# Segment sums of x by matmuls with tile loads, earlier stores of attention outputs, and a denser output projection at the end of attention

## Chip, core and metric

The kernel runs on one NeuronCore of a Trainium2 chip. The metric is the device time of one execution in microseconds (us). Differences of about 0.3% (3.8 us) or less can't be told from no change.

## What is computed

Two independent layers read 2048 tokens of width 1024 each, and their outputs stand side by side in the result.

```
# part A: a diagonal complex state space layer (S5)
Lam_bar = exp(dt * Lam)
Bu = einsum('bld,pd->blp', x, ((Lam_bar - 1) / Lam)[:, None] * Bmat)
for t in range(L):                       # a scan over 2048 tokens
    h = Lam_bar * h + Bu[:, t, :]
y = 2 * einsum('blp,dp->bld', hseq, Cmat).real + x * Dskip

# part B: attention with a recurrent memory; 64 segments of 32 tokens, 8 memory rows, 32 heads of 128
mem = mem0
for s in range(64):
    h = concatenate([mem, x[:, 32 * s:32 * s + 32]])      # 40 rows
    q, k, v = h @ Wq, h @ Wk, h @ Wv
    p = softmax(where(mask, q @ k.T * scale, -1e9))
    o = (p @ v) @ Wo
    mem = o[:, :8]; outs.append(o[:, 8:])
```

Part B's recurrence is broken up in the kernel: it forms a guess of each segment's memory from the segment's mean row of x, computes all segments at once with the guessed rows, compares at the end (`check`), and has a slow general path for inputs for which the guess would not do. The sums of x over each segment of 32 tokens, which this change concerns, feed that guess.

## The kernel before

The work runs in four stages on one core.

**Stage 1** (to about 335 us) interleaves two kinds of steps by the list that `steps()` (L949) makes. A "v" step (`v_x`, L470) multiplies 512 rows of part B's x with a 512-column block of Wv: 32 matmuls of 512 columns into psP, copied out by ScalarE (L89). An "s" step (`stage1`, L257), numbered n = 4 * pc + q from 0 to 31, is one block of part A's scan: 16 matmuls into psU, then on VectorE a product with tables (L268, which frees psU), a sum (L271), two scans (L276), a second product and sum (L287, L288), with ScalarE copies (L277) between and a small carry computed on GpSimd (L281 to L283). SP stores the result (a_hs, L289). After n = 6, 11, 16, 21, 26 and 30 no v step follows, so two scan steps meet there. There are two psU buffers and three psP buffers. In this stage the instructions of TensorE and SP keep the order in which the program writes them (`Pinned`, L54). The order on VectorE, ScalarE and GpSimd comes from a scheduler, except that instructions given to `keep_in_program_order` keep theirs among themselves.

**The segment sums** (`sum_x`, L414) are a generator whose pieces the stage 1 loop (L1028 to L1061) takes one at a time, one for each scan step from n = 3 on. x is viewed as 128 rows of 16 tokens, two rows for each segment. GpSimd issues 16 DMAs, token j of each row into one of two FP32 accumulators (j % 2); from the third on the DMA engines add while they write (L422). Two are issued per step, at n = 3 to 10. VectorE then adds the two accumulators (L427, at n = 11), ScalarE rounds the sum to BF16 (L429), VectorE forms the remainder (L431), and at n = 15 16 matmuls of 64 columns with the indicator `ind` (L107 to L111), two for each of 8 chunks of D, add the two rows of a segment. Four small VectorE instructions (L440 to L443) turn psR into xbar, the mean rows. The tile b_xr holds x rows for the first v step and then the accumulators; the rounded halves and a block of zeros (`fill`, L376) lie in the tile CT, which is loaded with C from n = 17 on.

**og** (L507) multiplies xbar with each Wv block: 32 matmuls of 64 columns into psR. For block 3 it runs at n = 17, and the load of Wv block 5 into the buffer that this frees follows it (L1050 to L1052). For later blocks both follow the block's last v step.

**Stage 2** (to about 460 us) is part A's output product and the guess.

**Attention** (to about 1027 us) goes over 16 head pairs, hp, of 11 units u each. The projections of q and k (`proj`, L587; 18 pieces per pair, 10 pieces ahead) run between the units. A unit has a front (scores on TensorE, exponential on ScalarE L647, mask on GpSimd L650) and a back (weighted values on TensorE, then VectorE L666 and L667 into b_ob), which runs two to three units later. b_ob has 44 blocks per head pair and is filled three blocks at a time. SP stores it to DRAM (b_on, b_tn) when the pair is complete; for the last pair alone (`early`, L671) the first groups are stored once 12 blocks are there. SP also loads the next pair's values (b_v) and the weights b_wq, b_wk. Pins are lifted here, so the scheduler orders all queues.

**Output projection**: when all projections are done, in the last eight units, one step (four matmuls of 512 columns) of `outproj_first` (L754) is taken after each unit (L1136). It has 64 steps: 18 for heads 0 to 23 of three row tiles, then heads 24 to 31, which need the last head pairs (tile b_ol3), and so on. The other three row blocks and the check follow.

Of the kernel before, what the change touches and what calls it, by code (L numbers as in the profile page):

```python
# [8 lines left out]
FP32 = mybir.dt.float32  # L9
BF16 = mybir.dt.bfloat16  # L10
I32 = mybir.dt.int32
ACT = mybir.ActivationFunctionType
ALU = mybir.AluOpType
# [26 lines left out]
EW = E + 8  # L40
# [53 lines left out]
def consts(k):  # L94
    nc, V, G = k.nc, k.V, k.G
    c = k.cst
    k.ident = c.tile([128, 128], BF16, name="ident")
    G.memset(k.ident[:], 1.0)
    G.affine_select(out=k.ident[:], in_=k.ident[:], compare_op=ALU.is_equal, fill=0.0, base=0,
                    pattern=[[-1, 128]], channel_multiplier=1)  # L100
    k.ones = c.tile([128, 1], BF16, name="ones")
    V.memset(k.ones[:], 1.0)
    k.hpb = c.tile([128, 1], FP32, name="hpb")
    k.hpe = c.tile([128, 1], FP32, name="hpe")
    V.memset(k.hpb[:], HALF_PI)
    k.S.activation(k.hpe[:], k.hpb[:], ACT.Exp)
    k.ind = c.tile([128, NSEG], BF16, name="ind")  # L107
    G.memset(k.ind[:], 1.0)
    for base, m in ((0, 1), (1, -1)):
        G.affine_select(out=k.ind[:], in_=k.ind[:], compare_op=ALU.is_ge, fill=0.0, base=base,  # L110
                        pattern=[[-2 * m, NSEG]], channel_multiplier=m)  # L111


def masks(k):
# [223 lines left out]
class PartB:  # L338
# [34 lines left out]
        k.V.tensor_copy(self.memT[:, :, 0:NMX + 1], self.m0T[:])  # L373
        k.V.memset(self.accR[:], 0.0)

    def fill(self, ct):  # L376
        k = self.k
        z = ct[0:32, 0, 2, 0:4 * EW]
        k.V.memset(z, 0.0)
        for hb in range(HB):  # L380
            k.SP.dma_start(self.vx[hb][64 + NMX:GX, :], z[0:GX - 64 - NMX, :])
            k.SP.dma_start(self.vx[hb][T + 32:NSLOT, :], z[0:32, :])
        for q in range(4):
            k.SP.dma_start(self.tn[q][NM:NR, 0:4 * EW], z[0:NR - NM, :])
            k.SP.dma_start(self.tn[q][NM:NR, 1024 - 4 * EW:1024], z[0:NR - NM, :])
# [13 lines left out]
        return [(64 + 1536, 1536, 384), (0, XMAIN, 64), (T - 64, T - 64, 64)]  # L399

    def load_x0(self, tmp, i):
        if i == 0:
            self.x0 = tmp.tile([128, 4, D], BF16, name="b_xr", bufs=1)
        self.k.SP.dma_start(self.x0[:, i, :], self.x[0][64 + 128 * i:192 + 128 * i, :])

    def turn_x0(self, i):

        k = self.k
        pt = k.ps("U", (128, 2, KC, 128), BF16)[:, 0, :, :]
        for c in range(KC):  # L410
            k.PE.transpose(pt[:, c, :], self.x0[:, i, c * 128:(c + 1) * 128], k.ident[:])
        k.copy("vs"[i % 2], self.xe[:, :, 128 * i:128 * i + 128], pt)

    def sum_x(self, tmp, ct):  # L414


        k = self.k; G = k.G
        acc = tmp.tile([128, 2, D], FP32, name="b_xr", bufs=1)
        rows = self.x[0].rearrange("(p j) d -> p j d", j=16)
        for j in range(16):  # L420
            op = {"accum_op": ALU.add} if j > 1 else {}
            k.tc.keep_in_program_order(G.dma_start(acc[:, j % 2, :], rows[:, j, :], **op))  # L422
            if j % 2:
                yield
        s = acc[:, 0, :]
        hl = ct[:, 0, 0:2, :]
        k.tc.keep_in_program_order(k.V.tensor_tensor(s, s, acc[:, 1, :], ALU.add))  # L427
        yield
        k.tc.keep_in_program_order(k.S.activation(hl[:, 0, :], s, ACT.Copy))  # L429
        yield  # L430
        k.tc.keep_in_program_order(k.V.tensor_tensor(hl[:, 1, :], s, hl[:, 0, :], ALU.subtract))  # L431
        yield
        yield
        p = k.ps("R")
        for c in range(KC):
            for i in range(2):
                k.PE.matmul(p[:, c * NSEG:(c + 1) * NSEG], hl[:, i, c * 128:(c + 1) * 128], k.ind[:], start=(i == 0), stop=(i == 1))
        pv = p[:].rearrange("p (c s) -> p c s", c=KC)
        ms = tmp.tile([128, KC], FP32, name="b_ms", bufs=1)
        k.V.tensor_reduce(ms[:], self.m0T[:], AX.X, ALU.add)  # L440
        k.V.tensor_scalar(self.xbar[:], pv, 1.0 / L, None, ALU.mult)
        k.V.tensor_tensor(ms[:], ms[:], pv[:, :, 0], ALU.add)
        k.V.tensor_scalar(self.xbar[:, :, 0], ms[:], 1.0 / L, None, ALU.mult)  # L443
        yield
# [209 lines left out]
    def att_back(self, blocks):  # L654

        k = self.k; PE, V = k.PE, k.V
        hp, b0, n = blocks[0][0], blocks[0][1], len(blocks)
        vt = self.vtile[hp]
        if b0 == 0:
            self.ob = self.p3a.tile([GW, 2 * NG, E], BF16, name="b_ob", bufs=2)  # L660
        o = k.ps(("O", "O", "R")[self.nback % 3], (128, 3, EO))
        self.nback += 1
        for i, (_, b, m, j) in enumerate(blocks):
            PE.matmul(o[:, i, 0:EV], m[:, j * GP:j * GP + 128], vt[:, b // 2, (b % 2) * EW:(b % 2) * EW + EV], start=True, stop=True)
        r = self.accR[0:GW, hp * 2 * NG + b0:hp * 2 * NG + b0 + n]
        V.reciprocal(r, o[0:GW, 0:n, E])  # L666
        V.tensor_tensor(self.ob[:, b0:b0 + n, :], o[0:GW, 0:n, 0:E], r.unsqueeze(2).to_broadcast([GW, n, E]), ALU.mult)  # L667
        q, cs = hp // 4, slice((hp % 4) * 256, (hp % 4) * 256 + 256)
        on, tn = self.on[q], self.tn[q]
        ov = self.ob[:].rearrange("p (g h) e -> p g (h e)", h=2)  # L670
        early = hp == HP - 1  # L671

        def rows(g0, g1):
            r = on[64 + GX * (g0 - 1):64 + GX * (g1 - 1), :].rearrange("(g p) n -> p g n", p=GX)
            k.SP.dma_start(r[:, :, cs], ov[0:GX, g0:g1, :])
        if early and b0 + n == 2 * GE:
            rows(1, GE)
            k.SP.dma_start(on[0:64, cs], ov[0:64, 0, :])
        if b0 + n == 2 * NG:
            del self.vtile[hp]  # L680
            if early:
                rows(GE, NG - 1)
            else:
                rows(1, NG - 1)
                k.SP.dma_start(on[0:64, cs], ov[0:64, 0, :])
            k.SP.dma_start(on[T - 64:T, cs], ov[0:64, NG - 1, :])
            k.SP.dma_start(tn[0:NTL, :].rearrange("(g j) n -> j g n", j=3)[:, :, cs], ov[GX:GW, :, :])
            k.SP.dma_start(tn[NTL:NM, cs], ov[64:64 + NMX, 0, :])
# [292 lines left out]
def kernel_main(tc, A_x, A_Lre, A_Lim, A_Bre, A_Bim, A_Cre, A_Cim, A_logdt, A_Dskip, B_x, B_mem0, B_Wq, B_Wk, B_Wv, B_Wo, out,  # L981
                force=False, dbg=None):
    with ExitStack() as ctx:
        k = K(tc, ctx)
# [15 lines left out]
        with pool("p1x", "right") as p1x, pool("p1", "right", 1) as p1:  # L1000
# [2 lines left out]
            warm(k, p1)  # L1003
            w0 = b.wl.tile([128, KC, 512], BF16, name="b_wv", bufs=2)
            b.load_wv_part(w0, 0, 0, 128, nc.scalar)
            for i in range(4):
                b.load_x0(p1, i)
                if i in (1, 2):
                    b.load_wv_part(w0, 0, 128 * i, (256, 512)[i - 1])
# [12 lines left out]
            b.init(p1)  # L1022
            a.tables(0)
            loads = [[(b, 2)], [(a, 1), (a, 2)], [(b, 3), (a, 3)]]
            sx = b.sum_x(p1, a.CT)
            tabs = {0: a.tabs}
            bts = {0: a.bt}
            for kind, pc, q in order[1:]:  # L1028
                if loads and kind == "v":
                    for o, n in loads.pop(0):  # L1030
                        o.load_x(n)
                if kind == "v":
                    b.v_x(pc, q, wv[pc])
                    if q == 3:
                        if pc > 3:
                            b.og(pc, wv[pc])
                        n = (pc + 2) if pc + 2 < PC else (2, 0)[pc + 2 - PC]
                        if pc != 3:
                            wv[n] = b.load_wv(n)
                    continue  # L1040
                a.tabs, a.bt = tabs[pc], bts[pc]
                n = 4 * pc + q
                if q == 2 and pc + 1 < PC:
                    a.load_b(pc + 1)
                    bts[pc + 1], a.bt = a.bt, bts[pc]
                if pc >= 4 and q == 1:
                    a.load_c(pc - 4)
                if n >= 3:
                    next(sx, None)
                if n == 17:  # L1050
                    b.og(3, wv[3])
                    wv[5] = b.load_wv(5)  # L1052
                a.stage1(pc, q)
                if q == 2 and pc + 1 < PC:
                    a.tables(pc + 1)
                    tabs[pc + 1] = a.tabs
                if n == 12:
                    masks(k)
                    check_consts(k)
                if n == 14:  # L1060
                    b.fill(a.CT)  # L1061
            k.pin.remove("PE")
        psu.close()
        k.psx = ctx.enter_context(tc.tile_pool(name="pss", bufs=1, space=PSUM, reuse_waits="tile"))
# [47 lines left out]
        for n, (hp, u) in enumerate(at):  # L1112
# [13 lines left out]
            if done == 18 * HP:  # L1126
                if first is None:
# [5 lines left out]
                    for h in range(0, H, 16):  # L1133
                        k.SP.dma_start(wo1[:, h:h + 16, :], b.Wo[:, h:h + 16, 512:D])
                    first = b.outproj_first()
                next(first)  # L1136
        p3.close()

# [88 lines left out]
```

## Time and profile before

| | |
|---|---|
| median of three runs | 1258.69 us (1256.14 to 1259.61) |
| the profiled execution | 1256.14 us, its span 1254.4 us |
| granted TensorE clock, mean | 0.997 |
| stage 1, scans under way (36.5 to 334.8 us) | 298.3 us, TensorE busy 288.1, VectorE 255.7 |
| attention, middle (490 to 1012 us) | 522.0 us, TensorE busy 521.6, VectorE 328.1 |
| end of attention (1012 to 1026 us) | 14.0 us, TensorE busy 13.0 |
| output projection (1026 to 1254 us) | 228.0 us, TensorE busy 223.2 |

PE stands for TensorE's matmuls, PEld for its weight loads, DVE for VectorE, ACT for ScalarE, POOL for GpSimd, SP for SyncE (here a queue that issues DMAs). Matmul durations in the rows are latencies, and they overlap: a 512-column matmul has a row of 379 ns, while sixteen follow each other in 3.45 us, 0.216 us apart. A wait is written behind a row in brackets: idle time before the instruction, and the instruction that ended it. The page's own list of the longest idle times before groups has these rows that bear on what follows:

```profile
L64 PE MATMUL psP<-b_wv,b_xe 128*128 128x512 bf16 (+2 forms) x1028 | 225.3, 375 | 7.5 <-ACT b_vst L89 5.8
L64 PE MATMUL psU<-a_xT,a_bt 128*128 128x512 bf16 x499 | 114.8, 380 | 3.6 <-DVE a_pr L268 2.9
b_xr<-in_B_x_dram POOLq DMA_DIRECT2D x16, 512.0 KB, 6.4
b_on<-b_ob SPq DMA_DIRECT2D x15, 960.0 KB
```

The first two are groups (count, busy us and mean ns, idle us before them); the last two are DMA issues (count, KB each, median us from issue to landing where known).

### The profile page before, as it was taken

The page shows a single profiled execution, that of the slowest core. Times are in us where ns is not written, and L with a number is a line of the kernel's source. Part 1 is how long each engine was busy: PE and PEld are TensorE (multiplying, and loading weights), DVE is VectorE, ACT ScalarE, POOL GpSimd, SP SyncE. Part 2 cuts the span into 40 slices and gives each one's busy share as a digit, 9 for nine tenths or more (in the row PEclk, how much of TensorE's full clock was granted, in tenths as well). Part 3 has the DMA queues.
Part 4 walks back from the last instruction along what each step waited for, and adds up shares of the span by engine and source line. Part 5 has one row for each costly group of instructions (what it writes and reads, how often), then busy time and mean ns, then how long its engine had stood idle before and what let it go on. Part 6 is the DMA issues. An engine that isn't in the chain of part 4 may idle for free.

```text
span 1254.4 us, 19885 instructions
## 1 busy us (share of the span) xinstructions
PE 1234.1 (98%) x8159; PEld 659.2 (53%) x8230; DVE 670.0 (53%) x1252; ACT 264.6 (21%) x632; POOL 290.7 (23%) x421
## 2 busy tenths in 40 slices
PE   9999989999999999999999999999999999999998
PEld 4444434444455555566665666565665654446444
DVE  4688699998811124666666666666666641001000
ACT  5344244443320000111211111111211210000000
POOL 4133422212332230222222222232223220000000
PEclk9999989999999999999999999999999999999999
DMA  9978623764698935475454454545474279507000
GB/s 254 230 218 216 179 90 94 194 164 134 166 329 254 276 104 134 122 206 143 107 143 107 114 137 103 129 101 120 95 159 92 60 222 221 125 17 152 17 17 27
DMA packets 316020, 181.00 MB, mean 144 GB/s; under 512 B 138650, under 2 KB 301326, under 8 KB 315926
## 3 DMA queue, kind: packets, MB, share of 16 engines
q1 hardware_dynamic: 291526, 143.75, 46.9%
q10 hardware_dynamic: 21072, 24.38, 5.8%
q0 software_dynamic: 3328, 11.56, 3.4%
q8 instruction: 65, 1.06, 0.4%
q14 instruction: 29, 0.24, 0.1%
HBM read 89.14 MB, written 53.17 MB: 113 GB/s over the span
## 4 chain that ended last, share of the span: by engine, by line
PE 93%; DVE 3%; DMA 3%; issue 1%; POOL 0%; ACT 0%; SPq 0%; DVEq 0%; POOLq 0%
PE psP L64 79%; PE psU L64 7%; PE psS L64 3%; PE psO L64 2%; PE psR L64 1%; DMA b_xr<-in_B_x_dram 1%; DVE a_pr L268 1%; DVE a_pr L276 1%; DMA wo<-in_B_Wo_dram 1%; DMA b_wv<-in_B_Wv_dram 1%; DVE a_pr L271 0%; DVE a_n L287 0%; POOL a_tt L281 0%; POOL a_nx L282 0%; SPq L64 0%
## 5 line engine op out<-in xcount | busy, mean ns | idle before, releaser
L64 PE MATMUL psP<-b_xe,b_wq 128*128 128x480 bf16 (+1 forms) x1280 | 247.7, 343 | 0.1
L64 PE MATMUL psP<-b_xe,b_wk 128*128 128x480 bf16 (+1 forms) x1280 | 247.7, 343 | 0.0
L64 PE MATMUL psP<-b_wv,b_xe 128*128 128x512 bf16 (+2 forms) x1028 | 225.3, 375 | 7.5 <-ACT b_vst L89 5.8
L650 POOL TENSOR_TENSOR b_m<-b_e,maskB 99x396 bf16<-99x396 bf16 x160 | 139.7, 873 | 334.4 <-ACT b_e L647 334.4
L647 ACT ACTIVATE b_e<-psS 99x396 bf16<-99x396 f32 x176 | 88.0, 500 | 532.8 <-PE psS L64 526.7
L64 PEld LDWEIGHTS <-b_wk 128*128 128x128 bf16 x1280 | 119.3, 98 | 94.3
L64 PEld LDWEIGHTS <-b_xe 128*128 128x128 bf16 x1056 | 102.1, 98 | 126.8 <-issue 8.8
L64 PEld LDWEIGHTS <-b_wq 128*128 128x128 bf16 x1280 | 118.6, 98 | 87.8
L91 DVE CAST b_k<-psP 128x480 bf16<-128x480 f32 (+1 forms) x192 | 97.4, 528 | 101.4 <-PE psP L64 101.4
L91 DVE CAST b_q<-psP 128x480 bf16<-128x480 f32 (+1 forms) x192 | 97.4, 528 | 93.0 <-PE psP L64 91.5
L64 PEld LDWEIGHTS <-b_ol 128*128 128x128 bf16 x864 | 84.2, 98 | 94.5
L64 PE MATMUL psU<-a_xT,a_bt 128*128 128x512 bf16 x499 | 114.8, 380 | 3.6 <-DVE a_pr L268 2.9
L64 PE MATMUL psP<-t,a_hl 128*128 128x512 bf16 x496 | 112.1, 379 | 0.8
L91 DVE CAST b_ost<-psP 128x512 bf16<-128x512 f32 (+1 forms) x17 | 11.5, 675 | 183.4 <-PE psP L64 182.4
L64 PE MATMUL psP<-wo,b_ol 128*128 128x512 bf16 (+1 forms) x440 | 91.9, 364 | 0.4
L64 PE MATMUL psP<-t,b_ol 128*128 128x512 bf16 x408 | 91.7, 379 | 0.4
L89 ACT ACTIVATE b_vst<-psP 128x512 bf16<-128x512 f32 x126 | 72.1, 588 | 75.5 <-PE psP L64 63.8
L667 DVE TENSOR_TENSOR b_ob<-psO,b_accR 99x384 bf16<-99x384 f32 x160 | 85.8, 553 | 2.0
L281 POOL TENSOR_SCALAR a_tt<-a_pr,a_tabf 128x1 f32<-128x1 f32 x48 | 34.3, 714 | 226.2 <-DVE a_pr L276 226.2
L64 PEld LDWEIGHTS <-a_bt 128*128 128x128 bf16 x512 | 49.8, 98 | 63.0 <-issue 4.3
L268 DVE TENSOR_TENSOR a_pr<-psU,a_tabf 128x2048 f32<-128x2048 f32 x32 | 73.0, 2282 | 13.5 <-PE psU L64 11.6
L64 PEld LDWEIGHTS <-a_hl 128*128 128x128 bf16 x512 | 49.0, 98 | 56.7
(204 smaller groups left out, 974.0 us busy)
## 6 DMA issues: line engine op xcount, KB each, us to landing
b_v<-b_vx SPq DMA_DIRECT2D x16, 1122.0 KB
b_wv<-in_B_Wv_dram SPq DMA_DIRECT2D x16, 1024.0 KB
b_on<-b_ob SPq DMA_DIRECT2D x15, 960.0 KB
b_vx<-b_vst ACTq DMA_DIRECT2D x24, 544.0 KB
a_hs<-a_h SPq DMA_DIRECT2D x32, 256.0 KB
b_xr<-in_B_x_dram POOLq DMA_DIRECT2D x16, 512.0 KB, 6.4
b_wog<-in_B_Wo_dram SPq DMA_DIRECT2D x4, 2048.0 KB
b_wq<-in_B_Wq_dram SPq DMA_DIRECT2D x16, 512.0 KB
```

Source lines behind the costliest of these rows:

```text
L64: r = f(*a, **kw)
L89: self.S.activation(out, in_, ACT.Copy)
L91: self.V.tensor_copy(out, in_)
L268: V.tensor_tensor(pr[:], u[:].unsqueeze(1).to_broadcast([128, 2, 2, TB]), view(t3, [[TB + 1, 2], [TB + 1, 2], [1, TB]]), ALU.mult)
L276: V.tensor_tensor_scan(w[:, j, :], rb, w[:, j, :], 0.0 if ini is None else ini[:, j:j + 1], ALU.mult, ALU.add)
L281: G.tensor_scalar(tt[:, j:j + 1], w[:, j, TB - 1:TB], t3[:, 1, TB:TB + 1], None, ALU.mult)
L647: k.S.activation(e[:], s[0:GW, :, :, 0:GW], ACT.Exp, scale=float(E) ** -0.5, accum_out=self.accE[0:GW, i:i + 1])
L650: k.G.tensor_tensor(m[0:GW, 0:4 * GP].rearrange("p (a b q) -> p a b q", a=2, b=2)[:, :, :, 0:GW], e[:], mask[0:GW, :, :].unsqueeze(2).to_b ...
L667: V.tensor_tensor(self.ob[:, b0:b0 + n, :], o[0:GW, 0:n, 0:E], r.unsqueeze(2).to_broadcast([GW, n, E]), ALU.mult)
```

## The change

The segment sums are made by TensorE. x is loaded as 16 tiles of 128 tokens (256 KB each) on SP's queue into four buffers of b_xr: four at n = 1, then one after each tile is used. From n = 3 to 10 two tiles are used per scan step: each is, chunk by chunk, the stationary operand of 8 matmuls whose moving operand is an indicator of 4 columns, one for each of the tile's four segments. xbar is made at n = 11 by the same four instructions. The accumulating DMAs and the instructions of L427 to L431 are gone. og for block 3 and the load of Wv block 5 follow that block's last v step, which comes after n = 13. The first v step's x rows are four tiles where they were one.

```
-    k.ind = c.tile([128, NSEG], BF16, name="ind")
-    G.memset(k.ind[:], 1.0)
-    for base, m in ((0, 1), (1, -1)):
-        G.affine_select(out=k.ind[:], in_=k.ind[:], compare_op=ALU.is_ge, fill=0.0, base=base,
-                        pattern=[[-2 * m, NSEG]], channel_multiplier=m)
+    k.ind = c.tile([128, 4], BF16, name="ind")
+    G.memset(k.ind[:], 0.0)
+    for j in range(4):
+        G.memset(k.ind[32 * j:32 * j + 32, j:j + 1], 1.0)
...
-        z = ct[0:32, 0, 2, 0:4 * EW]
+        z = tmp.tile([32, 4 * EW], BF16, name="b_xr", bufs=4)
...
-        if i == 0:
-            self.x0 = tmp.tile([128, 4, D], BF16, name="b_xr", bufs=1)
-        self.k.SP.dma_start(self.x0[:, i, :], self.x[0][64 + 128 * i:192 + 128 * i, :])
+        self.x0.append(tmp.tile([128, D], BF16, name="b_xr", bufs=4))
+        self.k.SP.dma_start(self.x0[i][:], self.x[0][64 + 128 * i:192 + 128 * i, :])
...
-        for j in range(16):
-            op = {"accum_op": ALU.add} if j > 1 else {}
-            k.tc.keep_in_program_order(G.dma_start(acc[:, j % 2, :], rows[:, j, :], **op))
-            if j % 2:
-                yield
-        s = acc[:, 0, :]
-        hl = ct[:, 0, 0:2, :]
-        k.tc.keep_in_program_order(k.V.tensor_tensor(s, s, acc[:, 1, :], ALU.add))
-        yield
-        k.tc.keep_in_program_order(k.S.activation(hl[:, 0, :], s, ACT.Copy))
-        yield
-        k.tc.keep_in_program_order(k.V.tensor_tensor(hl[:, 1, :], s, hl[:, 0, :], ALU.subtract))
-        yield
+        def load(t):
+            if t < TT:
+                xrs[t] = tmp.tile([128, D], BF16, name="b_xr", bufs=4)
+                k.SP.dma_start(xrs[t][:], self.x[0][t * 128:(t + 1) * 128, :])
+        for t in range(4):
+            load(t)
         yield
         p = k.ps("R")
-        for c in range(KC):
-            for i in range(2):
-                k.PE.matmul(p[:, c * NSEG:(c + 1) * NSEG], hl[:, i, c * 128:(c + 1) * 128], k.ind[:], start=(i == 0), stop=(i == 1))
+        for t in range(TT):
+            xr = xrs.pop(t)
+            for c in range(KC):
+                o = c * NSEG + 4 * t
+                k.PE.matmul(p[:, o:o + 4], xr[:, c * 128:(c + 1) * 128], k.ind[:], start=True, stop=True)
+            load(t + 4)
+            yield
...
-                        if pc > 3:
+                        if pc >= 3:
                             b.og(pc, wv[pc])
...
+                if n == 1:
+                    next(sx)
                 if n >= 3:
-                    next(sx, None)
-                if n == 17:
-                    b.og(3, wv[3])
-                    wv[5] = b.load_wv(5)
+                    for _ in range(2):
+                        next(sx, None)
```

Attention outputs are stored in two steps for head pairs 1 to 15, where it was pair 15 alone. And in the last eight units of attention two steps of the output projection are taken after each unit in place of one.

```
-        early = hp == HP - 1
+        early = hp > 0
...
                 next(first)
+                next(first)
```

More of the change, by code (lines that the diff above doesn't have):

```diff
@@ L374, in init, with fill @@
         k.V.memset(self.accR[:], 0.0)
-    def fill(self, ct):
+    def fill(self, tmp):
         k = self.k
-        z = ct[0:32, 0, 2, 0:4 * EW]
-        k.V.memset(z, 0.0)
+        z = tmp.tile([32, 4 * EW], BF16, name="b_xr", bufs=4)
+        k.V.memset(z[:], 0.0)
         for hb in range(HB):
@@ L410, in turn_x0, with sum_x @@
         for c in range(KC):
-            k.PE.transpose(pt[:, c, :], self.x0[:, i, c * 128:(c + 1) * 128], k.ident[:])
+            k.PE.transpose(pt[:, c, :], self.x0[i][:, c * 128:(c + 1) * 128], k.ident[:])
         k.copy("vs"[i % 2], self.xe[:, :, 128 * i:128 * i + 128], pt)
[L414 to L419, printed above, removed]
-        for j in range(16):
-            op = {"accum_op": ALU.add} if j > 1 else {}
-            k.tc.keep_in_program_order(G.dma_start(acc[:, j % 2, :], rows[:, j, :], **op))
-            if j % 2:
-                yield
-        s = acc[:, 0, :]
-        hl = ct[:, 0, 0:2, :]
-        k.tc.keep_in_program_order(k.V.tensor_tensor(s, s, acc[:, 1, :], ALU.add))
-        yield
-        k.tc.keep_in_program_order(k.S.activation(hl[:, 0, :], s, ACT.Copy))
-        yield
-        k.tc.keep_in_program_order(k.V.tensor_tensor(hl[:, 1, :], s, hl[:, 0, :], ALU.subtract))
-        yield
+    def sum_x(self, tmp):
+        k = self.k
+        xrs = {}
+        def load(t):
[4 more added lines that the diff above has]
+            load(t)
         yield
         p = k.ps("R")
-        for c in range(KC):
-            for i in range(2):
-                k.PE.matmul(p[:, c * NSEG:(c + 1) * NSEG], hl[:, i, c * 128:(c + 1) * 128], k.ind[:], start=(i == 0), stop=(i == 1))
+        for t in range(TT):
[5 more added lines that the diff above has]
+            yield
         pv = p[:].rearrange("p (c s) -> p c s", c=KC)
@@ L1005, in kernel_main @@
             b.load_wv_part(w0, 0, 0, 128, nc.scalar)
+            b.x0 = []
             for i in range(4):
@@ L1024, in kernel_main @@
             loads = [[(b, 2)], [(a, 1), (a, 2)], [(b, 3), (a, 3)]]
-            sx = b.sum_x(p1, a.CT)
+            sx = b.sum_x(p1)
             tabs = {0: a.tabs}
@@ L1034, in kernel_main @@
                     if q == 3:
-                        if pc > 3:
+                        if pc >= 3:
                             b.og(pc, wv[pc])
                         n = (pc + 2) if pc + 2 < PC else (2, 0)[pc + 2 - PC]
-                        if pc != 3:
-                            wv[n] = b.load_wv(n)
+                        wv[n] = b.load_wv(n)
                     continue
@@ L1060, in kernel_main @@
                 if n == 14:
-                    b.fill(a.CT)
+                    b.fill(p1)
             k.pin.remove("PE")
```

## The prediction

> **What bounds the kernel now.** I read the page's busy shares first, then a table of stages, then the waits of TensorE, and last the timeline around each long wait.
>
> ```profile
> PE 1234.1 (98%) x8159; PEld 659.2 (53%) x8230; DVE 670.0 (53%) x1252; ACT 264.6 (21%) x632; POOL 290.7 (23%) x421
> ```
>
> TensorE is busy for 1234.1 of 1254.4 us, so only 20.3 us of the span are not its work. The next view, busy time by stage, says where those lie: the stage of part A's scans (67 to 335 us), then the head pairs.
>
> ```profile
> 67.60:143.40 75.80, 75.43 (x346) 34.34 (x352) 61.69 (x54) 31.99 (x57) 30.07 (x44) 1.00 0.83 234
> 143.40:172.00 28.60, 19.84 (x82) 8.41 (x82) 24.35 (x20) 11.26 (x19) 6.05 (x7) 0.88 0.28 84
> 172.00:334.80 162.80, 161.91 (x864) 75.98 (x880) 146.98 (x130) 64.00 (x111) 38.53 (x69) 1.00 0.55 146
> ```
>
> Columns: length, busy time of PE, PEld, DVE, ACT, POOL, granted clock, DMA share, GB/s. One stretch of 28.6 us holds 8.76 us of idle TensorE, and its clock is 0.88; before and after it PE is 99.5% busy. The head pairs are tighter still: from 490 to 1012 us PE is busy for 521.63 of 522.00. The timeline of the bad stretch:
>
> ```profile
> 137.73 0.91 POOL L422 DMA_DIRECT2D b_xr<-in_B_x_dram  x1 [0.92 <-DMA b_xr<-in_B_x_dram]
> 139.58 0.87 POOL L422 DMA_DIRECT2D b_xr<-in_B_x_dram  x1 [0.95 <-DMA b_xr<-in_B_x_dram]
> 143.59 3.62 PE L64 MATMUL psU<-a_xT,a_bt 128*128 128x512 bf16 x16
> 146.64 1.23 DVE L427 TENSOR_TENSOR b_xr<-b_xr 128x1024 f32<-128x1024 f32 x1 [9.16 <-DMA b_xr<-in_B_x_dram]
> 147.78 2.28 DVE L268 TENSOR_TENSOR a_pr<-psU,a_tabf 128x2048 f32<-128x2048 f32 x1
> 150.12 3.61 PE L64 MATMUL psU<-a_xT,a_bt 128*128 128x512 bf16 x16 [2.91 <-DVE a_pr L268]
> 153.57 5.34 PE L64 MATMUL psP<-b_wv,b_xe 128*128 128x512 bf16 x23
> 164.71 3.57 PE L64 MATMUL psP<-b_wv,b_xe 128*128 128x512 bf16 x8 [5.79 <-ACT b_vst L89]
> 168.07 4.01 PE L64 MATMUL psU<-a_xT,a_bt 128*128 128x512 bf16 x16
> ```
>
> VectorE reaches L427, which adds the two accumulators, before the last accumulating transfer has landed, and stands for 9.16 us. Behind it in VectorE's order stands L268, which empties a psU buffer; PE wants that buffer at 147.2 and waits 2.91. The scans run late from there, ScalarE (whose table work waits for VectorE) empties psP late, and PE waits 5.79 more. After that wait matmuls of 512 columns run at half pace: eight take 3.57 us (eight at the usual 0.216 us spacing: 1.73), and by the chain of waits the next sixteen take 3.80 where others take 3.45.
>
> **The change, part by part.** (a) *The accumulating transfers, L427, L429 and L431 go.* The two waits are worth 2.91 + 5.79 = 8.70 us, and the slow matmuls (3.57 - 1.73) + (3.80 - 3.45) = 2.19 us. Would another wait take their place? Without L427 VectorE could start L268 when it fell idle, at 146.64 - 9.16 = 137.5, and free psU at 139.8, 7.4 us before PE asks. In the 162.8 us behind the stall VectorE is 147.0 busy and PE waits for nothing, and at the same meeting of two scan steps at 98.7 us PE ran 32 matmuls on end. So I take all of it: -10.89. Bounds: 0 if something else holds VectorE there, -10.89.
>
> (b) *128 matmuls of 4 columns come, 16 of 64 columns go.* These are on TensorE, which has no cover to give: each ns counts. Each new matmul has its own 128x128 weights. The trace has no 4-column matmul with full weights. Nearest row, the same weights with 64 columns:
>
> ```profile
> 203.46 1.10 PE L64 MATMUL psR<-b_xbar,b_wv 128*128 128x64 bf16 x32
> 204.40 1.89 PE L64 MATMUL psU<-a_xT,a_bt 128*128 128x512 bf16 x8
> ```
>
> From 203.46 to 204.40 are 32 of them: 29.4 ns each, though one weight load lasts 98 ns in its row, so loads overlap. Bounds: below, if spacing went on falling with columns as it does from 99 columns (four in 0.34 us, of which the last is 208 ns: 44 ns) to 64 (29.4), by 0.42 ns a column, 4 columns would take 4.4 ns, 0.6 us in all. Above, if 4 columns hide no load, 98 ns each, 12.5 us. I take 29.4, since a load must already keep that pace: 128 x 29.4 = 3.76 us. The 16 that go took 189.18 to 189.65: -0.47. Net +3.29, between +0.1 and +12.1.
>
> The Trainium skill, "TensorE: Matmul & The Clock Gate", section "LDWEIGHTS (loading the stationary operand)", gives a load its columns divided by 1.2 in ns, 107 ns for 128, and so speaks against this part: 13.7 us for 128 loads, and a sum near +1.4 us where mine is a gain. Its section "Weight-path perf modes" allows a faster load for 128 weights that aren't FP32; the 29.4 ns above side with that.
>
> (c) *Sixteen loads of 256 KB move to SP's queue, behind the a_hs stores there.* A load waits until TensorE is done with the tile four before it; behind it stand that step's a_hs store, the next b_wv load and the a_bt transposes. The stores are read only in stage 2, and the b_wv load for the next column block is queued ahead of the new pair (70.1 against 70.5 us). PE uses a pair two scan steps after its load is queued. From the SP timeline (stores at 69.7, 80.1, 91.6, 100.8, 113.5 us) and PE's steps, the margins are 18, 18, 10, 4, 9 and 14 us. The 4 belongs to the pair queued behind these:
>
> ```profile
> 101.15 2.47 SPq L64 DMA_TRANSPOSE a_bt<-in_A_B_re_dram  x1
> 103.67 4.68 SPq L64 DMA_TRANSPOSE a_bt<-in_A_B_im_dram  x1
> ```
>
> They end at 108.35, PE wants the tiles at 112.5. Landing times on POOL's queue are 5.7 us for 256 KB (a_xn) and 4.6 to 9.4 for the accumulating 512 KB; with 9.4 PE would wait 5.2 us. But the same two transposes took 1.55 and 1.31 us at 59.72, with no accumulating transfers in flight, which is how it will be here; 4.3 us more margin covers 5.7. I take 0, range 0 to 5.2.
>
> The skill's "DMA: Bandwidth & Descriptors", section "Anatomy of one DMA", has 2.0 us plus bytes over 436 GB/s, for 256 KB 2.6 us as an estimate, less than the row; by it the wait is 0 even with the slow transposes.
>
> (d) *og(3) and load_wv(5) move from step 17 to step 13.* The same 32 matmuls; xbar is made at step 11, two steps (some 20 us) ahead. The b_wv buffer comes free earlier, no PE wait hangs on it now. 0. The constant ind and the zero rows of fill are a few small instructions off the path, 0; the cover is that PE runs without them until step 3.
>
> (e) *Early stores for head pairs 1 to 14.* Fourteen more DMA issues, the same bytes. SP spends 0.3 to 2.5 us on a b_on issue, beside 253 us in which it waits for VectorE's b_ob. The early one will wait for the fourth b_ob group; behind it stands the b_wk load for the pair after next (713.47 us), which is read from about 746 (one pair lasts 33.78 us). 0, by that cover of 33 us; without it each us of lateness would cost 14.
>
> (f) *Two steps of output projection per attention unit.* The same matmuls, eight steps earlier. They fill PE's waits for GpSimd in the last units:
>
> ```profile
> 1018.48 0.23 PE L64 MATMUL psO<-b_v,b_m 128*128 128x129 bf16 x1 [0.20 <-POOL b_m L650]
> 1021.45 0.29 PE L64 MATMUL psO<-b_v,b_m 128*128 128x129 bf16 x2 [0.26 <-POOL b_m L650]
> 1025.68 0.29 PE L64 MATMUL psO<-b_v,b_m 128*128 128x129 bf16 x2 [0.44 <-POOL b_m L650]
> ```
>
> One step is four matmuls, 0.86 us, more than each wait: -0.90. What is late next: attention ends 8 x 0.86 = 6.9 us later, so do its last stores and the transposes of the next b_ol (issued 1034.3 to 1051.9, then to 1058.8). Their reader starts when the first block's 64 steps end, near 1075: 16 us of cover. The b_ol3 tile, needed at step 18, is issued at 1016.4 as now and read about 0.9 us sooner.
>
> Sum: -8.70 - 2.19 + 3.29 - 0.90 = -8.5 us. The profiled execution took 1256.14 us (span 1254.4), so 1247.6 on it; it is the lowest of the three runs, and their median is 1258.69, so 1250.2 for a median. I write 1250. With the bounds of (b): -11.7 to +0.3.
>
> **Rivals.** *The wait moves rather than goes* (0.15): the tight pair of (c) lands late by the whole 5.2 us and the slow clock comes with it (2.2): -8.5 + 7.4 = -1.1, 1257.6. For it: the 4 us margin, and VectorE 90% busy. Against: the quick transposes at 59.72.
>
> *Slower: weight loads don't hide under 4 columns* (0.09). If each pair of load and matmul takes the 195 ns of the one-column row (c_one), 128 make 25.0 us: -10.89 - 0.90 - 0.47 + 25.0 = +12.7, 1271. It breaks even at 96 ns a pair and is slower by 0.3% (3.8 us, about what a measurement of this kernel can tell from no change) from 126. Against: the 29.4 ns row. A late b_wk in each pair would need 0.9 us times fourteen to do the same (0.05).
>
> *The split stores do nothing* is part of the forecast, since they end no wait.
>
> **How the numbers follow.** Forecast 0.71, same 0.15, slower 0.14. The forecast's own range is 1247 to 1254 (the bound of -11.7, and +4 for part of a late tile). For eight in ten I go from 1246 to 1259, which takes in the first rival and leaves out the slow one. Faster 0.71, within 0.3% 0.15, slower 0.14.
>
> **What would show it.** No L427 and no VectorE wait on b_xr; PE's 2.91 and 5.79 gone and the clock 1.00 from 143 to 172; 128 rows psR<-ind,b_xr spaced near 29 ns, eight together 0.24 us; no PE wait on b_xr at steps 3 to 10; no POOL waits in the last units. Wrong, if the spacing is near 100 ns or more, or if psU or b_xr waits stand where these were.

## The result, and the profile after

The changed kernel took 1246.9 us (median of four runs, 1246.65 to 1247.2). The kernel before, run again beside it, took 1258.87 (four runs, 1256.14 to 1259.61). The ratio is 0.9909, with an interval of 0.9892 to 0.9926: faster by 0.9%, 12.0 us between the medians. The two profiled executions took 1256.14 and 1246.95 us, their spans 1254.4 and 1245.3, so 9.1 to 9.2 us lie between them, and that is the difference which the traces can explain.

The page of the changed kernel begins with the busy time of each engine and its instruction count:

```profile
PE 1234.2 (99%) x8270; PEld 662.5 (53%) x8342; DVE 667.7 (54%) x1250; ACT 263.4 (21%) x631; POOL 275.8 (22%) x407
```

TensorE is as busy as before (1234.1), in a span that is 9.1 us shorter: what went is idle time, while the new matmuls and the slow ones that are gone about even out. The table by stage says where. Columns as before: length, busy time of PE, PEld, DVE, ACT and POOL, granted clock, DMA share, GB/s.

```profile
67.60:143.40 75.80, 75.37 (x443) 35.84 (x450) 65.97 (x61) 31.50 (x55) 15.52 (x26) 1.00 0.59 177
143.40:172.00 28.60, 28.44 (x159) 13.50 (x161) 26.13 (x25) 12.66 (x22) 7.97 (x10) 1.00 0.19 68
172.00:334.80 162.80, 161.96 (x823) 75.41 (x838) 147.29 (x125) 64.31 (x113) 40.37 (x75) 1.00 0.57 149
...
1012.00:1026.00 14.00, 13.89 (x95) 7.40 (x95) 5.23 (x16) 2.37 (x8) 3.52 (x5) 1.00 1.08 294
```

The stretch from 143 to 172 us, which held 8.76 us of idle TensorE at a clock of 0.88, has 0.16 us at 1.00. In the window from 1012 to 1026 us, which held the end of attention before and now reaches some 5 us past it, TensorE went from 13.0 to 13.9 busy of 14. TensorE's row of time at the meeting of steps 11 and 12, the place of the long waits:

```profile
139.09 7.07 PE L64 MATMUL psP<-b_wv,b_xe 128*128 128x512 bf16 x32
145.99 7.07 PE L64 MATMUL psU<-a_xT,a_bt 128*128 128x512 bf16 x31
152.90 7.07 PE L64 MATMUL psP<-b_wv,b_xe 128*128 128x512 bf16 x31
```

No bracket stands behind any row: 32 matmuls of two scan steps run on end (one record of the 32 is missing), as the prediction took from the meeting at 98.7 us.

The new matmuls, eight for each x tile, two tiles a step:

```profile
66.82 0.54 PE L64 MATMUL psR<-ind,b_xr 128*128 128x4 bf16 x16
67.22 3.61 PE L64 MATMUL psU<-a_xT,a_bt 128*128 128x512 bf16 x16
```

The next matmul starts 0.40 us after the first of the sixteen: 25.2 ns each, with weights of its own for each. And SP's queue at the place where the prediction saw the thinnest margin:

```profile
101.57 1.48 SPq L64 DMA_TRANSPOSE a_bt<-in_A_B_re_dram  x1
103.10 1.32 SPq L64 DMA_TRANSPOSE a_bt<-in_A_B_im_dram  x1
104.52 1.97 SPq L64 DMA_DIRECT2D b_xr<-in_B_x_dram  x2
```

The transposes that took 2.47 and 4.68 us before take 1.48 and 1.32. The two tiles behind them are issued by 106.5 and read at 113.71; TensorE has no wait on b_xr. Its only listed wait in the whole profile is one of 1.3 us at the very start, which the kernel before has too.

### The profile page after: what moved, and what is told of

The parts are those of the page before. It is cut to its first block, busy times and chain, and to the rows that moved or that the text cites. A ratio compares the mean times of both kernels' runs of the same rounds, so it can differ in the third digit from the quotient of the medians.

```text
span 1245.3 us, 20124 instructions
## 1 busy us (share of the span) xinstructions
PE 1234.2 (99%) x8270; PEld 662.5 (53%) x8342; DVE 667.7 (54%) x1250; ACT 263.4 (21%) x631; POOL 275.8 (22%) x407
## 4 chain that ended last, share of the span: by engine, by line
PE 99%; issue 0%; DVE 0%
PE psP L64 82%; PE psU L64 9%; PE psS L64 3%; PE psO L64 2%; PE psR L64 2%; DVE b_xe L91 0%; DVE b_ost L91 0%; DVE a_n L962 0%; DVE hpb L105 0%; DVE ones L102 0%
```

## The experiments

All were timed in three rounds (the last two in five) beside the kernel before on the same chip, whose medians there were 1257.96 (e1 to e4), 1257.15 (e5 to e8) and 1257.2 (e9, e10). A value is a median with its runs' range. The changed kernel itself was timed in an earlier set, beside runs of the kernel before with a median of 1258.87, so differences to its 1246.9 compare runs that were not taken together, and so do those between experiments of different sets (three chips). Only e1 to e4, e5 to e8, and e9 and e10 stand side by side. All differences from here on that are below 3.8 us are small for this measurement; they are taken as real where the ranges of one set don't meet or where the traces show the same.

### Is it the transfers, or where VectorE meets them?

The theory of the prediction: the stall came from L427's place in VectorE's order, before the last accumulating transfer had landed. The rival: the accumulating transfers themselves hold the stage up, so that they have to go. This kernel is the one before with L427 taken after step 11's VectorE work; all accumulating transfers stay.

```
-                if n >= 3:
+                if n >= 3 and n != 11:
                     next(sx, None)
                 ...
                 a.stage1(pc, q)
+                if n == 11:
+                    next(sx)
```

> The kernel before, with one thing changed: the addition of the two accumulators (L427) is traced after scan step 11 instead of before it, so that it stands behind that step's work in VectorE's order; all accumulating transfers stay. Theory (the addition's place makes the stall): VectorE's wait of 9.16 us, TensorE's 2.91 and 5.79 us and the half-speed matmuls after them go, 10.9 us in all: the profiled time falls from 1256.1 to about 1245 to 1246, and the runs come closer together. Rival (the accumulating transfers themselves, or VectorE's load at 90%, hold up the scans): the waits stay, or appear one step later, and the time stays at 1254 to 1259.

Measured: 1248.97 (1247.79 to 1252.57), ratio 0.9932 (0.991 to 0.9955). The timeline of its VectorE, with L427 in its new place:

```profile
157.73 0.68 DVE L288 TENSOR_TENSOR a_h<-a_n 128x1024 bf16<-128x1024 bf16 x1
158.33 1.22 DVE L427 TENSOR_TENSOR b_xr<-b_xr 128x1024 f32<-128x1024 f32 x1
159.47 2.33 DVE L276 TENSOR_TENSOR_SCAN a_pr<-a_rr,a_pr 128x512 f32<-128x512 f32 x2
```

L427 starts 11.7 us later than in the kernel before, with no wait in front, and L268 no longer stands behind it. TensorE in the same stretch:

```profile
136.69 7.07 PE L64 MATMUL psP<-b_wv,b_xe 128*128 128x512 bf16 x31
143.60 7.07 PE L64 MATMUL psU<-a_xT,a_bt 128*128 128x512 bf16 x32
150.51 7.07 PE L64 MATMUL psP<-b_wv,b_xe 128*128 128x512 bf16 x31
...
203.59 1.89 PE L64 MATMUL psP<-b_wv,b_xe 128*128 128x512 bf16 x8 [1.45 <-ACT b_vst L89]
...
221.24 2.12 PE L64 MATMUL psP<-b_wv,b_xe 128*128 128x512 bf16 x9 [1.02 <-DMA b_wv<-in_B_Wv_dram]
```

Both long waits are gone with every transfer still there, so the transfers made the stall only through the place of one VectorE instruction. What remains is smaller: a wait for ScalarE's copies, and 1.02 us for the load of Wv block 5, which SP issues at 213.59, behind og at step 17. With these two waits the expectation was missed in part: the profiled run took 1247.79 where 1245 to 1246 was expected, and the runs lie no closer together (4.8 us apart). Moving that instruction alone in the kernel before is worth 9.0 us; the sums as changed bring 10.3 in the same set (e2 below), and the whole change 12.0 in its own.

### The parts at the end: one step or two, one store or more

Three variants of the changed kernel: the sums alone (attention as before), one projection step with the split stores, and two steps with the split store for the last pair alone.

```
e2 and e4:   -        early = hp > 0
             +        early = hp == HP - 1
e2 and e3:   -                next(first)      (one of the two)
```

> The segment sums as changed, but the output stores and the one output projection step per unit as before. Theory: stall and slow matmuls go (-10.9 us), the matmuls cost 128 x 25.2 ns less the 0.47 us of the old ones (+2.8): about 8 us under the profiled 1256.1, 1248, and some 1 to 2 us above the changed kernel's 1246.9. Rival (a good part of the 12 us comes from the stores or the denser end of attention): 1250 or more.

> The changed kernel with one output projection step per unit, as before. Theory: TensorE waits for GpSimd in the last units again, three or four waits of 0.2 to 0.5 us; 0.9 to 1.8 us above the changed kernel: 1247.8 to 1248.7. Rival (the waits were hidden by something else): 1246.9.

> The changed kernel with only the last head pair stored in two steps, as before. Theory (the split stores end no wait): 1246.9, within 0.4 us. Rival (they spare TensorE the 0.3 us of idle time between 490 and 1012 us, or let the last transposes start earlier): 0.3 to 1 us longer.

| | split stores of pairs 1 to 14 | without them |
|---|---|---|
| two steps | 1246.9 (the change) | 1245.94 (1245.86 to 1246.06), e4 |
| one step | 1248.4 (1248.34 to 1249.03), e3 | 1247.66 (1247.16 to 1248.09), e2 |

The second projection step is worth 1.5 (with the split stores) and 1.7 us (without); the split stores cost 1.0 and 0.7 us. The 1.7 and the 0.7 compare runs of one set whose ranges don't meet; the 1.5 and the 1.0 compare with the changed kernel's own set. Neither the theory nor the rival written down for e4 foresaw that it would be the faster one. Ratios to the kernel before: e2 0.9909 (0.9886 to 0.9932), e3 0.9918 (0.9895 to 0.9941), e4 0.9897 (0.9875 to 0.992). The sums alone are 10.3 us below the kernel before in the same set of runs.

Where the steps' gain comes from is seen in e3's TensorE at the end of attention:

```profile
1008.54 0.28 PE L64 MATMUL psO<-b_v,b_m 128*128 128x129 bf16 x2
1009.02 0.23 PE L64 MATMUL psO<-b_v,b_m 128*128 128x129 bf16 x1 [0.20 <-POOL b_m L644]
...
1011.51 0.22 PE L64 MATMUL psO<-b_v,b_m 128*128 128x129 bf16 x1
1011.99 0.29 PE L64 MATMUL psO<-b_v,b_m 128*128 128x129 bf16 x2 [0.26 <-POOL b_m L644]
...
1015.39 0.39 PE L64 MATMUL psO<-b_v,b_m 128*128 128x129 bf16 x4
1016.22 0.29 PE L64 MATMUL psO<-b_v,b_m 128*128 128x129 bf16 x2 [0.43 <-POOL b_m L644]
```

The three waits for GpSimd are those of the kernel before. What they cost is more than the brackets say. Such matmuls follow each other 0.057 us apart (six in 0.34 in the rows of the changed kernel below), so the third of the first group would have started at 1008.65 and started at 1009.02: 0.37 us lost where 0.20 is written, since a bracket counts from the end of the row before, and the overlap of the two rows is lost as well. The others lose 0.42 and 0.60; together 1.4 us, near the 1.5 to 1.7 measured (e2's profile also has a wait of 0.54 us at 492.84 that e4's lacks, so not all of the 1.7 need be the step's). In the changed kernel the same matmuls stand without a bracket:

```profile
1020.58 0.50 PE L64 MATMUL psO<-b_v,b_m 128*128 128x129 bf16 x6
1020.92 0.28 PE L64 MATMUL psR<-b_v,b_m 128*128 128x129 bf16 x2
1021.03 1.89 PE L64 MATMUL psP<-t,b_wv 128*128 128x512 bf16 x8
```

The price of the split stores is not on any engine. The last VectorE copy of the changed kernel, and below it that of e4:

```profile
1239.32 0.42 DVE L91 CAST b_ost<-psP 128x256 bf16<-128x256 f32 x1 [6.24 <-PE psP L64]
```

```profile
1239.25 0.42 DVE L91 CAST b_ost<-psP 128x256 bf16<-128x256 f32 x1 [6.24 <-PE psP L64]
```

All computation ends within 0.07 us of each other, but the spans end at 1245.3 and 1244.2. The waits of SP's own queue show one at the program's last lines, in the kernel before, the changed kernel and e4, in this order (sum, times, longest):

```profile
SPq L1161 <- SPq L1161: 1.2, 2, 0.7
```

```profile
SPq L1156 <- SPq L1156: 2.8, 1, 2.8
```

```profile
SPq L1156 <- SPq L1156: 1.4, 2, 0.9
```

From the end of the last copy to the end of the span, called the closing here, are 5.6 us in the changed kernel, 5.4 in e3, 4.5 in e2 and e4, and 3.7 to 3.8 in the kernel before and e1 (one profile each).

### Is it the stores, or the number of instructions on SP?

The theory: the closing grows with the number of DMA instructions on SP, wherever they stand. The rival: the stores of attention themselves (late data, late landing) lengthen it. This kernel is e4 with fourteen more DMAs in stage 1, a thousand microseconds before the end: fourteen a_hs stores written as two each.

```
-        k.SP.dma_start(self.hs[tb][:, pc, :, :], h[:])
+        if 12 <= 4 * pc + tb < 26:
+            k.SP.dma_start(self.hs[tb][:, pc, 0, :], h[:, 0, :])
+            k.SP.dma_start(self.hs[tb][:, pc, 1, :], h[:, 1, :])
+        else:
+            k.SP.dma_start(self.hs[tb][:, pc, :, :], h[:])
```

> The changed kernel with only the last head pair stored in two steps (1245.9), and instead 14 of the 32 a_hs stores of stage 1 issued in two halves, so that SP again has 14 DMA instructions more, but not in attention. Theory (the 1 us that the split output stores cost lies behind the last computation and hangs on SP's longer instruction stream): about 1246.9, with 5.4 to 5.6 us from the last VectorE copy to the end instead of 4.5. Rival (it is the output stores themselves, their DMAs or semaphores): 1245.9.

Measured: 1246.82 (1246.71 to 1246.99), 0.88 us above e4 and equal to the changed kernel. Its SP wait at the end:

```profile
SPq L1160 <- SPq L1160: 2.9, 1, 2.9
```

The closing is 5.6 us again, and its last copy starts at 1239.19. So the stores of attention are not needed for it; fourteen more DMA instructions on SP do it by themselves. Nor does it go by the packets that the DMAs moved: the changed kernel has 223 more than e4 and e6 has 2015 more, with 5.6 us in both. Why more instructions on SP make the closing longer isn't shown. The pages give no sign of more pieces of instructions being brought in: their two queues of the kind "instruction" moved 66 and 30 packets in the changed kernel and in e6, 66 and 31 in e4.

### The price of the 4-column matmuls

Each of the 128 matmuls is issued three times and writes the same product each time. If TensorE has slack in this stage, the 256 more cost less than 256 x 25.2 ns = 6.45 us.

```
-                k.PE.matmul(p[:, o:o + 4], ..., k.ind[:], start=True, stop=True)
+                for _ in range(3):
+                    k.PE.matmul(p[:, o:o + 4], ..., k.ind[:], start=True, stop=True)
```

> The changed kernel with each of the 128 matmuls of 4 columns issued three times into the same place (each with its own weight load; the result is the same). Theory (TensorE has no cover to give in this stage, and one pair of load and matmul costs its spacing of 25.2 ns): 256 x 25.2 ns = 6.45 us longer, 1253.4, about twice the price of the sums. Rival (VectorE, 90% busy, leaves TensorE some slack there): clearly less than 6.45 us.

Measured: 1253.32 (1252.97 to 1253.73), 6.42 us above the changed kernel, ratio to the kernel before 0.9968 (0.9957 to 0.9979); that compares two sets, but the traces say the same: from scan step 0 to the last VectorE copy its profile is 6.50 us longer than the changed kernel's. Its timeline at step 3:

```profile
66.95 1.34 PE L64 MATMUL psR<-ind,b_xr 128*128 128x4 bf16 x48
68.16 3.18 PE L64 MATMUL psU<-a_xT,a_bt 128*128 128x512 bf16 x13
```

48 in 1.21 us: 25.2 ns again. Each ns of them counts in full.

### The place of og and of the Wv load

The changed kernel with og for block 3 and the load of Wv block 5 back at step 17.

```
-                        if pc >= 3:
+                        if pc > 3:
                             b.og(pc, wv[pc])
...
+                if n == 17:
+                    b.og(3, wv[3])
+                    wv[5] = b.load_wv(5)
```

> The changed kernel with og for block 3 and the load of Wv block 5 back at step 17. The prediction took this move at nothing: 1246.9, no wait of TensorE on b_wv. Rival (the load had little time to spare before, and the move is part of the gain): a TensorE wait on b_wv of 1 us or more near 220 us, 1248.

Measured: 1247.2 (1246.97 to 1247.91), 0.3 us above the changed kernel, with overlapping ranges, and no TensorE wait on b_wv. The move is worth nothing that these runs can tell; in e1, where SP and TensorE meet a little otherwise, the same late load cost the 1.02 us shown above.

### A version with the accumulating transfers

e1 with the load and og at step 16 and two projection steps: L427 held, no new matmuls, no split stores.

```
-                if n == 17:
+                if n == 16:
                     b.og(3, wv[3])
...
                 next(first)
+                next(first)
```

> The kernel before with the accumulating transfers, L427 traced after scan step 11 (as in the run that showed 1249.0), og for block 3 and the load of Wv block 5 at step 16 instead of 17, and two output projection steps per unit. Theory (what is left over in that run is TensorE's 1.0 us wait for this b_wv load, and the waits of the last units, 1.4 us): about 1246.5, and with no 4-column matmuls perhaps below the changed kernel. Rival (accumulating transfers leave waits that move about from run to run): 1248 or more, with a spread of some us.

Measured: 1245.18 (1245.0 to 1245.62), ratio 0.9903 (0.9887 to 0.992). It is the fastest here, 1.7 us below the changed kernel's median from the other set and 1.6 to 2.0 below e6 and e8 in the same one, though still with TensorE waits that the changed kernel lacks:

```profile
PE psP L64 <- ACT b_vst L89: 1.6, 1, 1.6
PE psU L64 <- DMA b_xr<-in_B_x_dram: 0.9, 1, 0.9
PE psP L64 <- DMA b_wv<-in_B_Wv_dram: 0.5, 1, 0.5
```

The Wv wait at 221 us is gone (the 0.5 is at 9.8 us). It saves the 2.8 us net of the new matmuls, and its closing is 3.75 us long.

### The start-up

Kernels whose first x rows lie in one tile (before, e1, e7) start scan step 0 on TensorE at 36.5 to 36.6 us, those with four tiles at 35.5 to 35.9. In the former the second tile's transposes wait 0.2 to 0.9 us for a load; but two with four tiles have that wait as well, e2 (0.80) and e6 (0.64), and start at 35.86 and 35.51. Two kernels try whether the tiling is the reason: e9 is e4 with the four x0 tiles as slices of one tile again (in the empty C tile), e10 is e7 with the first two as tiles of their own.

```
e9:   -        self.x0.append(tmp.tile([128, D], BF16, name="b_xr", bufs=4))
      +        (self.x0 = a.CT[:, 1, 0:4, :], loaded slice by slice)
e10:  -            self.x0 = tmp.tile([128, 4, D], BF16, name="b_xr", bufs=1)
      +        if i < 2:
      +            self.x0.append(tmp.tile([128, D], BF16, name="b_x0", bufs=2)[:])
```

> The kernel of e4_last_early (1245.94), except that the four x tiles of the first v step are slices of one tile again, here in the still empty C tile. Theory that one tile makes the second tile's transposes wait for a later load: the 0.9 us wait of TensorE on x before the second eight transposes (6.08 us in the kernels with one tile) comes back, the first psU row of scan step 0 stands near 36.5 instead of 35.5 to 35.9, and the time is about 0.7 us higher, 1246.6. Rival, that the start-up differs for another reason (which loads are in flight, where the tile lies): no such wait, 1245.9.

> The kernel of e7_acc_og16 (accumulating transfers kept, L427 behind step 11's VectorE work, og at step 16, two projection steps, early stores for the last pair alone; 1245.18), with the first two x tiles of the first v step as tiles of their own. If tile granularity makes the start-up wait: the 0.9 us wait at 6.08 us goes, psU of scan step 0 starts about 0.7 us sooner, 1244.5. If the start-up differs for another reason: 1245.2.

Measured: e9 1246.71 (1246.23 to 1247.79), e10 1245.48 (1245.36 to 1245.51). The timeline of e9 (the tile is called t there):

```profile
4.43 0.61 PE L64 MATMUL psU<-ident,t 128*128 128x128 bf16 x8
5.74 0.62 PE L64 MATMUL psU<-ident,t 128*128 128x128 bf16 x8 [0.70 <-DMA t<-in_B_x_dram]
...
35.77 3.62 PE L64 MATMUL psU<-a_xT,a_bt 128*128 128x512 bf16 x16
```

The wait came back, but step 0 starts at 35.77, no later than in e4 (35.82): the wait costs nothing there, and e9's 0.8 us more come from elsewhere (its profile has a wait of 0.60 us for ScalarE at 345.64). That its time is near the 1246.6 expected is luck. In e10 the wait shrank to 0.40 us, and step 0 starts at 36.69, no sooner. So the tiles are not the reason.

The traces show the place. In the kernel before and in the changed one these are the 16 matmuls of 256 columns with the second part of Wv, and step 0:

```profile
9.73 1.91 PE L64 MATMUL psP<-b_wv,b_xe 128*128 128x256 bf16 x16 [0.55 <-DMA b_wv<-in_B_Wv_dram]
...
36.54 3.62 PE L64 MATMUL psU<-a_xT,a_bt 128*128 128x512 bf16 x16
```

```profile
8.93 1.91 PE L64 MATMUL psP<-b_wv,b_xe 128*128 128x256 bf16 x16
...
35.74 3.62 PE L64 MATMUL psU<-a_xT,a_bt 128*128 128x512 bf16 x16
```

From the one to the other are 26.81 us in every kernel but e3 (27.18, with a wait of its own), and in before, e1, e7 and e10 alone the chain that ended last goes through the load of Wv that SP issues at 2.84 us; it lands at 9.7 to 9.8 us there. In the other kernels these matmuls start at 8.70 to 9.08 and do not wait for it. Why the load lands later in the four is open; the accumulating transfers, first issued at 68.9 us, can't be the reason.

## Why the prediction came out as it did

The time lay 3.1 us under the predicted 1250, 0.1 us under the forecast's own range (1247 to 1254) and inside the wider one (1246 to 1259), and the forecast's mechanism is the one that acted. On the profiled executions its sum was -8.5 us and the spans give -9.1, but that nearness is partly luck: four terms were off and two parts not foreseen, and they cancel.

**(a), the stall, right in cause and slightly short.** e1 shows the cause by itself: the transfers kept, VectorE's wait gone, both TensorE waits gone, mean clock 1.000. The term -8.70 took the two brackets as they stand. By the count of lost starts that e3's rows show, they cost 3.08 (the first psU matmul could have started at 147.04 and started at 150.12) and 5.96 us, 9.04 together. The slow matmuls' time went as well: none of the three stretches from 67 to 335 us has a clock under 1.00. The prediction's 2.19 for it is a little high, since 3.57 us is a row that holds the last matmul's latency, set against a spacing. From start to start the 8 and the 16 took 3.36 and 3.85 us where 1.73 and 3.45 are usual: 2.03 lost.

**(b), the new matmuls, right in kind, the size 17% too high.** 25.2 ns each where 29.4 were taken, 3.2 us for 128 where 3.76 stood, net of the 16 that went +2.76. e5 shows that the term counts in full. The bound from one load's 98 ns row was far off: the new loads, 96 ns each in their rows, overlap. The Trainium skill's formula for a load ("TensorE: Matmul & The Clock Gate", section "LDWEIGHTS (loading the stationary operand)"; 107 ns for 128 columns as an estimate by it) is not what such a pair costs in these runs, about a quarter of it. The same page's section "Back-to-back issue gap" has a floor of about 25 ns for up to 64 columns, in a table for the matmul without its load; the 25.2 ns of the pairs with 4 columns is as short, while the 29.4 at 64 columns lies above it.

**(c), the tile loads on SP, right, with one thing missed.** The reason given, that the transposes would be quick without accumulating transfers beside them, is what the SP rows show, and e1 (which keeps those transfers) has them slow again, 2.98 and 4.31 us. The skill's section that the prediction quotes here, on the anatomy of one DMA, is on DMAs that GpSimd issues; the tile loads go out on SP, and no row here shows how long they take to land. What was missed stands under (e).

**(d), og and the Wv load moved, right at nothing** in this kernel (e8), with a thin margin: the cover is gone in e1 and costs 1.0.

**(e), the split stores, wrong at nothing.** They cost 0.7 to 1.0 us. The step that failed is "0, by that cover of 33 us": the cover hides the waits, and it did, since TensorE's work ends at the same time with and without them. But the term looked for a cost only among engines that wait, and the cost was in the closing, where more SP instructions make it longer (e6). The sixteen tile loads of (c) seem to pay the same way: 4.3 to 4.5 us of closing in e2, e4 and e9 against 3.7 in the kernel before, though no run took that part out alone.

**(f), two projection steps, mis-sized.** -0.90 was the sum of three brackets; e2 against e4 and e3 against the change give -1.7 and -1.5. The brackets leave out the lost overlap; counted by starts the three waits are 1.4.

**Not foreseen:** 0.8 us at the start, since the first matmuls no longer wait for a load of Wv (why it lands sooner is open), and a wait of TensorE early in attention that the changed kernel does not have, put down to no other engine:

```profile
501.67 0.50 PE L64 MATMUL psO<-b_v,b_m 128*128 128x129 bf16 x6 [0.37 <-issue]
```

Put together on the spans: -9.04 - 2.03 + 2.76 - 1.4 - 0.8 - 0.37 + 1.83 (closing 5.56 against 3.73) = -9.05, against -9.1 measured.

**The step from the profiled run to the median failed by most of what the number missed.** The prediction added 2.55 us because the median of before lay that much above its profiled run, as if the changed kernel would have the same distance. It has none: its runs lie within 0.55 us, at a mean granted clock of 0.999 to 1.000. The runs of before range over 3.5 us beside the changed kernel, over 5.7 beside e1 to e4, there with a clock from 0.994 (the run of 1262.99) to 0.997 (one of 1257.36), and over 1.8 and 1.7 in the two later sets. So the medians are 12.0 apart where the profiled executions are 9.2 apart, and against the medians that before had in the other sets, 1257.15 to 1257.96, the same 1246.9 would be 10.3 to 11.1 below. That the half-pace stretch behind the stall varies from run to run may be the reason, but that is not shown: e1, without that stall, still had runs of 1251.07 and 1252.57 at clocks of 0.998 and 0.997.

**The rivals.** The wait did not move: there is no b_xr wait. A load and its matmul took 25.2 ns together, far from the 96 at which that rival breaks even. And the accumulating transfers need not go for the gain: e7 keeps them and is faster.

## What to carry to other kernels

Before replacing a mechanism that an engine waits for, move the waiting instruction in that engine's order: one VectorE instruction that starts 11.7 us later brought 9.0 us where the whole rewriting brought 12.0 in its own set, and the version built on it (e7) came out 1.7 us under the rewritten one. Size a wait by the start that the pipelined instruction would have had, not by the printed idle time, which here was 0.17 us short at each wait. And cost added DMA instructions at the end of the program as well as where they stand.

## What the runs showed of the hardware

- Matmuls of 4 columns, each with its own 128x128 BF16 weights, followed each other at 25.2 ns, with 48 on end as with 16, while the row of one of these loads lasts 96 ns.
- Fourteen more DMA instructions on SP lengthened the closing by 0.9 to 1.1 us (4.5 to 5.4 or 5.6 us from the last copy to the end of the span), whether they stood in stage 1 or in attention.
- The same pair of DMA transposes took 1.48 to 1.50 and 1.30 to 1.32 us to issue in the eight kernels without accumulating transfers and 2.10 to 2.98 and 4.31 to 5.04 in the four with them.
- After 2.91 us of idle TensorE the next 16 matmuls kept the full pace (3.45 us); after 5.79 us the next 8 took 3.57 us, where such a row of 8 has 1.89 in e1.
